# Second-transform points interleaved and rows moved in pairs, in a fused FFT convolution and recurrent-memory kernel

## Chip, cores and metric

The kernel runs on one core of a Trainium2 chip. The metric is the device time of one execution in microseconds (us); lower is better. Five runs of the kernel before have a median of 2174.39 us (2169.2 to 2178.17).

## What is computed

Two independent results stand side by side in the output, `out[0, s, 0:1024]` and `out[0, s, 1024:2048]`. Part A is a long convolution; part B is a recurrent attention with memory. Only A's data movement is changed. The reference, cut down:

```python
# A: S = 2048 positions, D = 1024 channels
k_shift = sum(k_pad[:, t:t+S, :] * shift_k[:, 3-t] for t in range(4))   # 4-tap causal filter
kv  = k_shift * v
y   = irfft(rfft(kv, 4096) * rfft(ssm_k, 4096))[:S]                     # long convolution per channel
a   = q * (y + kv * ssm_D)
# B: for each of 64 segments of 32 positions, with 8 memory rows in front
h = concat([mem, x[seg]]);  q, k, v = h@Wq, h@Wk, h@Wv                  # 32 heads of 128
o = softmax(mask(q k^T * scale)) v @ Wo;  mem = o[:8];  out = o[8:]
```

## The kernel before, in words

**Order of the work.** `b_kernel` opens with B's preparations and calls A inside them (L632, `run_a`). A has three stages; in between and after them B's weights are loaded and projections that don't depend on the recurrence are computed. The recurrent loop over 64 segments (L859) comes last, under a hand-written order (`tc.manual_schedule()`, L805). Outside that block the framework chooses the order of each engine's instructions; in the trace, for example, weight loads of L541 stand between A's stores of L211 on the SP queue.

**A's transform.** Position `s = 16 p + r`, with `p` the partition (0 to 127) and `r` the row within it (0 to 15). The 4096-point transform is split: a first transform over `p` (a 128x128 matmul with `F1h`), then a second one over 32 points, made of the 16 rows `r` and a half `h` (0 or 1, the two matrices `F1h[0]`, `F1h[1]`). Between the two, the data go through DRAM, because the second needs another partition layout: `SK1` (the kernel's transform) and `SU1` (the data's), both `[128, 32, 1024]` bf16, with frequency `m` outermost and the 32 points in the middle. In the text before, point `n = 16 h + r`.

**Stage 1** (L214 to L244), 16 iterations `t`, one row each. PE transposes eight blocks of `ssm_k` (L218), ACT copies them (`kt`, L220), `stage1(kt)` makes 4 matmuls (L208), ACT casts two PSUM tiles of 1024 columns into `s_sb` (L210, three buffers), and SP stores `s_sb` (512 KB) to `SK1` (L211). Meanwhile SP loads row `t` of k (`K0`, 256 KB, five buffers, L225), POOL loads row `t` of v (L228; for `t < 8` into the eight slots `pw` that later hold weights, afterwards into two `Vt` buffers), DVE makes seven operations (four products with `SH`, three sums, the product with v: L237 to L243), and `stage1(u)` does as above into `SU1`. The filter needs rows `t-3` to `t`; rows before 0 are rows 13 to 15 of the partition above, which are loaded into `Kx` (two buffers) each time that they are used, six times in all, each as a POOL memset of partition 0 and two loads of 112 and 15 partitions (L60 to L63). When a `pw` slot is free again, a weight chunk of 512 KB is loaded into it (`group`, L541), and for streamed chunks POOL copies it to the DRAM tensor `WS` (L543).

**Between 1 and 2**, `stage1_done` (L477) places twelve resident chunks `Wmid` and runs the projection `dense(0, 0)` on PE (L584).

**Stage 2** (L352 to L363): 17 sets, each gathering 256 KB pieces of `SK1` and `SU1` with the 32 points of four frequencies on 128 partitions (L276), two half-units of matmuls with `Mre`, `Mim`, complex products on DVE and POOL, the inverse with `Nre`, `Nim`, and a store to `SZ` (L284), laid out as `SK1`. After each half-unit `fill()` (L618) puts in one step of B's projections.

**Stage 3** (L369 to L382), 16 iterations: SP loads `zt` (both halves of point row `t`, 512 KB, L372) and row `t` of q (256 KB, L378; four buffers each), PE makes 4 matmuls with `G2h` into one of three PSUM tiles (L375), DVE multiplies with q (L380) into `ot` (three buffers), POOL stores the row (L381), and `fill()` follows.

**After A**, B's value projections (`vb_ps`, L701) run on PE while their weights and the resident ones come in, and their results go to DRAM (`VBD`, L705). Then the loop starts; it streams weights with loads of 512 KB in 4 KB runs (`wring<-WS`, L661).

**The layout that the change is about.** A row of 1024 bf16 is 2 KB. With `n = 16 h + r`, the two halves of a point row lie 32 KB apart in DRAM, so each partition's 4 KB in `sb` is stored as two runs of 2 KB:

```python
nc.sync.dma_start(scratch.rearrange("m (h r) d -> r m h d", h=2)[t], sb[:])
```

Of the kernel before, what the change touches and what calls it, by code (L numbers as in the profile page):

```python
# [9 lines left out]
BF = mybir.dt.bfloat16  # L10
F32 = mybir.dt.float32
I32 = mybir.dt.int32
ACT = mybir.ActivationFunctionType
ALU = mybir.AluOpType
# [17 lines left out]
def a_kernel(ctx: ExitStack, tc, q, k, v, shift_k, ssm_k, ssm_D, outa, slot4, slot16, stage1_done, fill):  # L32
    nc = tc.nc
    S, D = 2048, 1024
    NP = 34
    NS = 17
# [5 lines left out]
    SZ = dram.tile([128, 32, D], BF, name="SZ")  # L42
# [6 lines left out]
    Nre = const.tile([128, NS, 128], BF, name="Nre")  # L49
    Nim = const.tile([128, NS, 128], BF, name="Nim")  # L50

    def rows_view(ap2d, t):
        return ap2d.rearrange("(p r) d -> r p d", r=16)[t]

    def load_rows(dst, src2d, t, lag, eng):
        c = t - lag
        if c >= 0:
            eng.dma_start(dst, rows_view(src2d, c))
        else:
            nc.gpsimd.memset(dst[0:1, :], 0.0)  # L60
            rv = rows_view(src2d, 16 + c)
            eng.dma_start(dst[1:113, :], rv[0:112])
            eng.dma_start(dst[113:128, :], rv[112:127])  # L63

    with ExitStack() as c1:
        cw = c1.enter_context(tc.tile_pool(name="a_cw", bufs=1, side="right"))
        io = c1.enter_context(tc.tile_pool(name="a1_io", bufs=2, side="right"))
        k0pool = c1.enter_context(tc.tile_pool(name="a1_k0", bufs=5, side="right"))
        wk = c1.enter_context(tc.tile_pool(name="a1_wk", bufs=3, side="right"))
        ps_big = c1.enter_context(tc.tile_pool(name="a1_ps", bufs=2, space=PSUM))  # L70
        ps_t = c1.enter_context(tc.tile_pool(name="a1_pst", bufs=2, space=PSUM))
# [66 lines left out]
        p_odd = icol("p_odd", ALU.bitwise_and, 1)  # L138
# [37 lines left out]
        for hf in range(4):  # L176
            pt = ps_big.tile([128, 1024], F32, tag="big", name="sh_ps")
            for e in range(2):
# [4 lines left out]
        p_mod32 = icol("p_mod32", ALU.bitwise_and, 31)  # L183
        p_div64 = icol("p_div64", ALU.arith_shift_right, 6)
        p_x = icol("p_x", ALU.arith_shift_right, 5, ALU.bitwise_and, 1)
        nx = cw.tile([128, 1], F32, name="nx")
        nc.vector.tensor_tensor(out=nx[:], in0=p_mod32[:], in1=p_div64[:], op=ALU.mult)
        phr = cw.tile([128, 1], F32, name="phr")
        nc.vector.tensor_scalar(out=phr[:], in0=p_x[:], scalar1=-1024.0, scalar2=1024.0, op0=ALU.mult, op1=ALU.add)
        phi = cw.tile([128, 1], F32, name="phi")  # L190
# [8 lines left out]
        w_f = cw.tile([128, NS], F32, name="w_f")  # L199
        nc.vector.tensor_scalar(out=w_f[:], in0=w_i[:], scalar1=kp[:, 0:1], scalar2=None, op0=ALU.add)  # L200
        nc.vector.tensor_tensor(out=aN0, in0=w_f[:].unsqueeze(2).to_broadcast([128, NS, 32]),
                                in1=kcol_f[:, 0:32].unsqueeze(1).to_broadcast([128, NS, 32]), op=ALU.mult)
        def stage1(u_tile, t, scratch):
            sb = wk.tile([128, 2, 1024], BF, tag="s1_sb", name="s1_sb")
            for h in range(2):
                pt = ps_big.tile([128, 1024], F32, tag="big", name="s1_ps")
                for hf in range(2):
                    nc.tensor.matmul(pt[:, hf * 512:(hf + 1) * 512], lhsT=F1h[h][:, :],  # L208
                                     rhs=u_tile[:, hf * 512:(hf + 1) * 512], start=True, stop=True)
                nc.scalar.copy(sb[:, h, :], pt[:])  # L210
            nc.sync.dma_start(scratch.rearrange("m (h r) d -> r m h d", h=2)[t], sb[:])  # L211

        ktiles = {}
        for t in range(16):  # L214
            pt = ps_t.tile([128, 1024], BF, tag="ktp", name="k_tp")
            for db in range(8):
                src = KS[:, db, :].rearrange("p (n r) -> p r n", r=16)[:, t, :]
                nc.tensor.transpose(pt[:, db * 128:(db + 1) * 128], src, ident[:])  # L218
            kt = wk.tile([128, 1024], BF, tag="kt", bufs=2, name="kt")
            nc.scalar.copy(kt[:], pt[:])  # L220
            if t == 0:
                nc.vector.tensor_tensor(out=kt[0:1, :], in0=kt[0:1, :], in1=Drow[0:1, :], op=ALU.add)
            stage1(kt, t, SK1)
            K0 = k0pool.tile([128, 1024], BF, tag="K0", name="K0")
            load_rows(K0, k, t, 0, nc.sync)  # L225
            ktiles[t] = K0
            Vt = slot4()[:, 0:1024] if t < 8 else io.tile([128, 1024], BF, tag="Vt", name="Vt")[:]
            load_rows(Vt, v, t, 0, nc.gpsimd)  # L228
            acc = wk.tile([128, 1024], BF, tag="uacc", bufs=2, name="uacc")
            for li, lag in enumerate((3, 2, 1, 0)):  # L230
                if t - lag >= 0:
                    Kl = ktiles[t - lag]
                else:
                    Kl = io.tile([128, 1024], BF, tag="Kx", name="Kx")
                    load_rows(Kl, k, t, lag, nc.sync)
                if li == 0:
                    nc.vector.tensor_tensor(out=acc[:], in0=Kl[:], in1=SH[:, lag, :], op=ALU.mult)  # L237
                else:
                    pr = wk.tile([128, 1024], BF, tag="prod", bufs=2, name="prod")
                    nc.vector.tensor_tensor(out=pr[:], in0=Kl[:], in1=SH[:, lag, :], op=ALU.mult)  # L240
                    nc.vector.tensor_tensor(out=acc[:], in0=acc[:], in1=pr[:], op=ALU.add)
            u = wk.tile([128, 1024], BF, tag="u", bufs=2, name="u")
            nc.vector.tensor_tensor(out=u[:], in0=acc[:], in1=Vt, op=ALU.mult)  # L243
            stage1(u, t, SU1)  # L244

        for x, (M, n) in enumerate(((Mre, nxr), (Mim, nxi))):
            aM = phases(x).rearrange("p (a b) -> p a b", b=32)
            nc.vector.tensor_scalar(out=aM, in0=v_i, scalar1=p_mod32[:, 0:1], scalar2=n[:, 0:1], op0=ALU.mult, op1=ALU.add)
            nc.vector.tensor_scalar(out=aM, in0=aM, scalar1=4095, scalar2=None, op0=ALU.bitwise_and)
            for (r0, c0) in [(0, 0), (64, 32)]:  # L250
                act_sin(M[r0:r0 + 64, :, c0:c0 + 32], aM[r0:r0 + 64], 12, r0)
            nc.gpsimd.memset(M[32:64, 0, :], 0.0)
# [112 lines left out]
    with ExitStack() as c3:  # L365
        io = c3.enter_context(tc.tile_pool(name="a3_io", bufs=4, side="right"))
        wk = c3.enter_context(tc.tile_pool(name="a3_wk", bufs=3, side="right"))
        ps_big = c3.enter_context(tc.tile_pool(name="a3_ps", bufs=3, space=PSUM))
        for t in range(16):  # L369
            pt = ps_big.tile([128, 1024], F32, tag="big", name="y_ps")  # L370
            zt = io.tile([128, 2, 1024], BF, tag="zt", name="zt")
            nc.sync.dma_start(zt[:], SZ.rearrange("m (h r) d -> r m h d", h=2)[t])  # L372
            for hf in range(2):
                for h in range(2):
                    nc.tensor.matmul(pt[:, hf * 512:(hf + 1) * 512], lhsT=G2h[h][:, :],  # L375
                                     rhs=zt[:, h, hf * 512:(hf + 1) * 512], start=(h == 0), stop=(h == 1))
            qt = io.tile([128, 1024], BF, tag="qt", name="qt")
            load_rows(qt, q, t, 0, nc.sync)  # L378
            ot = wk.tile([128, 1024], BF, tag="ot", name="ot")
            nc.vector.tensor_tensor(out=ot[:], in0=pt[:], in1=qt[:], op=ALU.mult)  # L380
            nc.gpsimd.dma_start(rows_view(outa, t), ot[:])  # L381
            fill()  # L382


# [732 lines left out]
```

## Time and profile before

| what | us |
|---|---|
| median of five runs | 2174.39 |
| the profiled execution | 2176.56 |
| its span, first to last instruction | 2173.6 |
| stage 1: first and last store issued (L211) | 20.2 and 115.6 |
| stage 3: first load and last store issued (L372, L381) | 291.9 and 348.8 |
| first weight load of the loop on SP (L661) | 433.0 |
| DVE operation of 128x1024 in stage 1 (L241) | 0.680 |
| ACT cast of 128x1024 in stage 1 (L210) | 1.037 |
| store to SK / SU, issue to landing, median | 4.6 / 5.1 |
| load of a row of k / q / zt, issue to landing, median | 6.0 / 6.5 / 8.5 |

How to read the views: "busy" is the time in which an engine executes; the figure in brackets after it is the number of instructions. In a timeline line the first number is the start and the second the duration, and the square bracket at its end gives the idle time before it and what ended it. "SPq" and "POOLq" are the instruction queues of SP and POOL, which issue DMAs in order: an issue that waits holds up all behind it. In the DMA view q1 holds the transfers issued by SP, q10 those of ACT, q0 those of POOL; the share is the time that packets took, over 16 engines and the window. Pipelined operations overlap a little, so the step from one ACT cast to the next is about 0.91 us and from one DVE operation to the next about 0.60 us.

### The profile page before, as it was taken

The page shows a single profiled execution, that of the slowest core. Times are in us where ns is not written, and L with a number is a line of the kernel's source. Part 1 is how long each engine was busy: PE and PEld are TensorE (multiplying, and loading weights), DVE is VectorE, ACT ScalarE, POOL GpSimd, SP SyncE. Part 2 cuts the span into 40 slices and gives each one's busy share as a digit, 9 for nine tenths or more (in the row PEclk, how much of TensorE's full clock was granted, in tenths as well). Part 3 has the DMA queues.
Part 4 walks back from the last instruction along what each step waited for, and adds up shares of the span by engine and source line. Part 5 has one row for each costly group of instructions (what it writes and reads, how often), then busy time and mean ns, then how long its engine had stood idle before and what let it go on. Part 6 is the DMA issues. An engine that isn't in the chain of part 4 may idle for free. (4 is left out here: it accounts for less than half of the span.)

```text
span 2173.6 us, 81452 instructions
## 1 busy us (share of the span) xinstructions
PE 1737.9 (80%) x35636; PEld 929.5 (43%) x35636; DVE 872.7 (40%) x2686; ACT 648.2 (30%) x1139; POOL 436.7 (20%) x1131
## 2 busy tenths in 40 slices
PE   4688989777888878888788788888888878888776
PEld 2232334334444444444444444444444444444444
DVE  9927752123333333333333333333333333333332
ACT  8935521122222222222222222222222222222221
POOL 4013532301111111111111112111111111111111
PEclk9899999989999999999999999999999999999999
DMA  9998879999999999999999999999999999999996
GB/s 327 340 336 305 278 288 389 286 367 394 392 365 368 394 373 391 389 391 397 390 394 396 393 393 389 392 382 383 389 383 382 389 390 392 396 390 393 393 369 259
DMA packets 262572, 804.63 MB, mean 370 GB/s; under 512 B 52204, under 2 KB 52236, under 8 KB 262215
## 3 DMA queue, kind: packets, MB, share of 16 engines
q1 hardware_dynamic: 229880, 725.84, 87.7%
q0 software_dynamic: 27120, 63.11, 8.5%
q10 hardware_dynamic: 5216, 10.49, 1.3%
q8 instruction: 278, 4.55, 0.9%
q14 instruction: 78, 0.64, 0.1%
HBM read 739.92 MB, written 62.39 MB: 369 GB/s over the span
## 5 line engine op out<-in xcount | busy, mean ns | idle before, releaser
L893 PEld LDWEIGHTS <-rec 128*32 128x32 bf16 x12351 | 324.8, 96 | 479.6 <-issue 256.8
L893 PE MATMUL acc<-wring,rec 128*32 128x512 bf16 (+1 forms) x3777 | 376.3, 387 | 142.8 <-DMA wring<-WS 125.4
L902 ACT CAST qkv_sb<-acc 128x512 bf16<-128x512 f32 x384 | 224.8, 585 | 666.7 <-PE acc L893 666.7
L979 PEld LDWEIGHTS <-OT 128*32 128x32 bf16 x8192 | 217.9, 97 | 179.1 <-issue 152.0
L979 PE MATMUL yacc<-wring,OT 128*32 128x256 bf16 x3072 | 154.8, 276 | 98.0 <-DMA wring<-WS 58.7
L893 PE MATMUL acc<-Wmid,rec 128*32 128x512 bf16 x3072 | 227.5, 386 | 0.0
L893 PE MATMUL acc<-Wres,rec 128*32 128x512 bf16 x2816 | 222.5, 382 | 0.0
L995 DVE COPY KT<-tps 128x512 bf16<-128x512 bf16 x64 | 27.2, 425 | 307.3 <-PE tps L908 307.3
L839 PEld LDWEIGHTS <-OTB 128*16 128x16 bf16 x4096 | 105.0, 90 | 102.7 <-issue 92.4
L965 ACT CAST OT<-OTp 128x512 bf16<-128x512 f32 x128 | 74.9, 585 | 245.6 <-PE OTp L957 245.6
L966 DVE CAST OTB<-OTp 128x128 bf16<-128x128 f32 x128 | 37.3, 292 | 266.5 <-ACT OT L965 266.5
L794 POOL DMA_DIRECT2D rec<-REC x64 | 37.4, 585 | 521.5 <-issue 267.6
L745 DVE TENSOR_SCALAR wring<-OTp 128x384 int32<-128x384 int32 x126 | 112.2, 891 | 53.5 <-PE acc L893 45.1
L893 PE MATMUL acc<-pw,rec 128*32 128x512 bf16 x1536 | 130.4, 382 | 0.0
L869 POOL COPY KT<-rec 128x128 bf16<-128x128 bf16 x128 | 38.6, 302 | 437.6 <-PE SB L917 435.1
L854 POOL DMA_DIRECT2D out_dram<-YB x128 | 73.1, 577 | 232.8 <-DVE YB L852 228.2
L923 DVE TENSOR_REDUCE mx<-SB 128x5 f32<-128x200 f32 x128 | 47.1, 368 | 172.6 <-PE SB L917 172.6
L839 PE MATMUL SB<-wring,OTB 128*16 128x256 bf16 x1488 | 79.2, 275 | 36.3 <-DVE SB L818 30.2
L908 PE MATMUL tps<-ident,qkv_sb 128*128 128x128 bf16 x1024 | 101.2, 221 | 8.0 <-ACT qkv_sb L902 0.2
L908 PEld LDWEIGHTS <-qkv_sb 128*128 128x128 bf16 x1024 | 62.7, 97 | 104.8 <-ACT qkv_sb L902 64.8
L979 PE MATMUL yacc<-Wlate,OT 128*32 128x256 bf16 x2048 | 105.7, 275 | 2.1 <-issue 1.3
L1035 ACT CAST Y<-yacc 128x256 bf16<-128x256 f32 x64 | 23.8, 372 | 241.0 <-PE yacc L979 225.5
(231 smaller groups left out, 2675.6 us busy)
## 6 DMA issues: line engine op xcount, KB each, us to landing
wring<-WS SPq DMA_DIRECT2D x1216, 512.0 KB, 7.4
rec<-REC POOLq DMA_DIRECT2D x64, 192.0 KB, 6.2
SK<-s_sb SPq DMA_DIRECT2D x16, 512.0 KB, 4.6
SU<-s_sb SPq DMA_DIRECT2D x16, 512.0 KB, 5.1
Kg<-SK SPq DMA_DIRECT2D x32, 256.0 KB, 4.5
Ug<-SU SPq DMA_DIRECT2D x32, 256.0 KB, 6.1
REC<-stage POOLq DMA_DIRECT2D x16, 512.0 KB, 8.6
zt<-SZ SPq DMA_DIRECT2D x16, 512.0 KB, 8.5
```

What stands on the lines that cost most here:

```text
L745: nc.vector.tensor_scalar(out=dst, in0=src, scalar1=0, scalar2=None, op0=ALU.bitwise_or)
L794: nc.gpsimd.dma_start(rec[:], REC[:, s, :])
L839: nc.tensor.matmul(self.acc[32 * dq:32 * dq + W, x - o:y - o], lhsT=self.OTB[:, c, 4 * g + i, :], rhs=r, start=first and not self.seeded, ...
L854: nc.gpsimd.dma_start(bass.AP(outb.tensor, outb.offset + (SEG * NB * self.b + NX) * 2048 + 256 * dq, [[2048 * SEG, NB], [2048, 8], [1, 256 ...
L869: nc.gpsimd.tensor_copy(KT[:, :, :, 32:40], KBs[:, 128 * g:128 * g + 128].rearrange("p (c i t) -> p i c t", c=4, i=4))
L893: nc.tensor.matmul(self.acc[32 * c:32 * c + 32, x - 512 * c:y - 512 * c], lhsT=hT[:, kc, :], rhs=r, start=(kc == 0 and x == 512 * c), stop ...
L902: nc.scalar.copy(sb[:], self.acc[:])
L908: nc.tensor.transpose(tp[:, i * 128:(i + 1) * 128], sb[:, i * 128:(i + 1) * 128], ident[:])
L923: nc.vector.tensor_reduce(out=mx[:], in_=S, op=ALU.max, axis=AX.X)
L965: nc.scalar.copy(OT[:], o_view[:, :, :, 0:32])
L966: nc.vector.tensor_copy(OTB[:, :, 4 * g:4 * g + 4, 8 * j:8 * j + 8], o_view[:, :, :, 32:40])
L979: nc.tensor.matmul(yacc[32 * dq:32 * dq + 32, x - o:y - o], lhsT=OT[:, c, i, :], rhs=r, start=(h == 0 and x == o), stop=(h == 31), tile_po ...
```

## The change

It has five parts.

1. The 32 points of the second transform are numbered `n = 2 r + h`. The stores of stage 1 and the loads of stage 3 now see one run of 4 KB per partition. The matrices `M` and `N` are built with the permuted numbers (`p_n2`, `kn2`); this adds three small DVE operations for `p_n2`'s base, one more for `p_n2` and one for `kn2`, and no operation later on. The gathers and scatters of stage 2 keep their shapes.
2. k is loaded two rows at a time into `K0` of 4 KB (four buffers of two rows for five of one).
3. v is loaded two rows at a time: rows 0 to 11 into six `pw` slots, rows 12 to 15 into two `Vt` buffers of 4 KB. Slots 6 and 7 are no longer used for v.
4. q is loaded two rows at a time (two buffers of two rows for four of one), and the output is stored two rows at a time after the odd row (two buffers of two for three of one). In the output tensor the rows lie 4 KB apart, so its runs stay 2 KB.
5. The shifted rows 13 to 15 are loaded once into `Kx` `[128, 3, 1024]` with one memset and two loads, ahead of the loop.

The diff's core:

```diff
+        p_n2 = icol("p_n2", ALU.arith_shift_right, 1, ALU.bitwise_and, 15)
+        nc.vector.scalar_tensor_tensor(out=p_n2[:], in0=p_odd[:], scalar=16.0, in1=p_n2[:], op0=ALU.mult, op1=ALU.add)
+        nc.vector.scalar_tensor_tensor(out=kn2[:], in0=odd_f[:, 0:32], scalar=16.0, in1=half_f[:, 0:32], op0=ALU.mult,
+                                       op1=ALU.add)
...
-            nc.sync.dma_start(scratch.rearrange("m (h r) d -> r m h d", h=2)[t], sb[:])
+            nc.sync.dma_start(scratch.rearrange("m (r h) d -> r m h d", h=2)[t], sb[:])
...
+        Kx = cw.tile([128, 3, 1024], BF, name="Kx")
+        nc.gpsimd.memset(Kx[0:1], 0.0)
+        kx_src = k.rearrange("(p r) d -> p r d", r=16)[:, 13:16, :]
+        nc.sync.dma_start(Kx[1:113], kx_src[0:112])
+        nc.sync.dma_start(Kx[113:128], kx_src[112:127])
+        ktiles = {c: Kx[:, c + 3, :] for c in (-3, -2, -1)}
...
-            K0 = k0pool.tile([128, 1024], BF, tag="K0", name="K0")
-            load_rows(K0, k, t, 0, nc.sync)
-            ktiles[t] = K0
-            Vt = slot4()[:, 0:1024] if t < 8 else io.tile([128, 1024], BF, tag="Vt", name="Vt")[:]
-            load_rows(Vt, v, t, 0, nc.gpsimd)
+            if t % 2 == 0:
+                K0 = k0pool.tile([128, 2048], BF, tag="K0", name="K0")
+                nc.sync.dma_start(K0[:], pair_rows(k, t))
+                ktiles[t], ktiles[t + 1] = K0[:, 0:1024], K0[:, 1024:2048]
+                Vp = slot4(t // 2) if t < 12 else io.tile([128, 2048], BF, tag="Vt", name="Vt")
+                nc.gpsimd.dma_start(Vp[:], pair_rows(v, t))
...
-            nc.sync.dma_start(zt[:], SZ.rearrange("m (h r) d -> r m h d", h=2)[t])
+            nc.sync.dma_start(zt[:], SZ.rearrange("m (r h) d -> r m h d", h=2)[t])
...
-            qt = io.tile([128, 1024], BF, tag="qt", name="qt")
-            load_rows(qt, q, t, 0, nc.sync)
-            ot = wk.tile([128, 1024], BF, tag="ot", name="ot")
-            nc.vector.tensor_tensor(out=ot[:], in0=pt[:], in1=qt[:], op=ALU.mult)
-            nc.gpsimd.dma_start(rows_view(outa, t), ot[:])
+            if t % 2 == 0:
+                qt = io.tile([128, 2048], BF, tag="qt", bufs=2, name="qt")
+                nc.sync.dma_start(qt[:], pair_rows(q, t))
+                ot = wk.tile([128, 2048], BF, tag="ot", bufs=2, name="ot")
+            half = slice(1024 * (t % 2), 1024 * (t % 2) + 1024)
+            nc.vector.tensor_tensor(out=ot[:, half], in0=pt[:], in1=qt[:, half], op=ALU.mult)
+            if t % 2:
+                nc.gpsimd.dma_start(outa.rearrange("(p r) d -> p r d", r=16)[:, t - 1:t + 1, :],
+                                    ot[:].rearrange("p (r d) -> p r d", r=2))
```

## Prediction

> **What bounds the kernel now.** First the page: how long each kind of work lasts. Its second part cuts the span into 40 slices of 54 us.
>
> ```profile
> span 2173.6 us, 81452 instructions
> ...
> PE   4688989777888878888788788888888878888776
> ...
> DMA  9998879999999999999999999999999999999996
> ```
>
> From the ninth slice on (433 us) runs B's loop, with DMA at 9 throughout. No line of it is changed, so all that can move lies in the first 435 us: a fifth of the span, and only the part of it that sets when the loop starts. Next the windows of the stages, with busy time per engine, the granted clock, DMA share and GB/s:
>
> ```profile
> 32.00:116.10 84.10, 54.55 (x247) 22.92 (x245) 73.43 (x132) 75.38 (x85) 6.82 (x13) 0.86 0.96 337
> 116.10:144.50 28.40, 28.40 (x124) 12.37 (x123) 3.46 (x5) 5.85 (x10) 0.00 (x0) 0.94 0.91 329
> 144.50:288.00 143.50, 127.33 (x692) 42.71 (x692) 109.34 (x190) 79.63 (x151) 63.40 (x62) 0.96 0.83 285
> 288.00:348.00 60.00, 46.72 (x208) 19.57 (x206) 24.85 (x25) 5.27 (x9) 17.04 (x26) 0.89 0.98 367
> 348.00:405.00 57.00, 57.00 (x266) 25.85 (x265) 9.08 (x16) 12.87 (x22) 18.05 (x25) 1.00 1.02 359
> ```
>
> The columns after the length are PE, PEld, DVE, ACT, POOL. Stage 1 (first line) is ACT's: 75.4 of 84.1 us; DVE has 73.4, but its last product ends at 105.3 us and ACT's last copy at 116.05. Then PE is full in the dense projection, nearly full in stage 2, has 13 us of gaps in stage 3, and is full again to 405 us. So what a stage gives up is passed on to the loop's start, unless DMA holds it: in stage 3 and after it DMA is at 0.98 to 1.02. What fills ACT's 8.7 us of idle time in stage 1, and DVE's, is in the waits:
>
> ```profile
> ACT s_sb L210 <- DMA SU<-s_sb: 6.1, 6, 1.8
> ACT s_sb L210 <- issue: 1.1, 1, 1.1
> ...
> DVE prod L240 <- POOL coli L505: 1.4, 1, 1.4
> DVE uacc L237 <- DMA Kx<-in_A_k_dram: 1.0, 1, 1.0
> DVE prod L240 <- DMA K<-in_A_k_dram: 1.0, 2, 0.8
> DVE prod L240 <- DMA Kx<-in_A_k_dram: 1.0, 1, 1.0
> ```
>
> ACT waits six times, up to 1.8 us, for a store of `s_sb` to land before the buffer can be written again. Three buffers are filled in about 7.3 us, of which 1.8 is the filling, so a store may take 5.5 us; the median is 5.1. Which stores are late is seen on SP's queue:
>
> ```profile
> 75.86 0.56 SPq L58 DMA_DIRECT2D K<-in_A_k_dram  x1
> 76.51 0.80 SPq L541 DMA_DIRECT2D pw<-in_B_Wk_dram  x1
> 78.01 0.52 SPq L211 DMA_DIRECT2D SU<-s_sb  x1
> ```
>
> The store issued at 78.0 stands behind 256 KB of k and 512 KB of weights; ACT waits for it until 84.49 (1.44 us lost). Each of the six late stores has a load of 512 KB shortly in front.
>
> Stage 3, by its waits (PE's line, then DVE's):
>
> ```profile
> PE y_ps L375 <- DMA zt<-SZ: 7.8, 6, 2.2
> ...
> DVE ot L380 <- DMA qt<-in_A_q_dram: 10.5, 2, 9.1
> ```
>
> Is DMA full there because runs are short? The DMA view of 20 us of stage 3 (2 KB runs), then of 100 us of the loop (4 KB runs): packets, MB, share.
>
> ```profile
> q1 hardware_dynamic: 3024, 5.90, 77.5%
> ```
>
> ```profile
> q1 hardware_dynamic: 9668, 35.19, 92.0%
> ```
>
> Per MB that is 0.775 x 320 / 5.90 = 42.0 and 0.920 x 1600 / 35.19 = 41.8 us of one engine: as good as equal. The packet records of the trace are kinder: the median 2 KB packet on SP's queue took 84 ns, a 4 KB packet 159, so two short ones cost 168: 5% more.
>
> **What the Trainium skill says.** "DMA: Bandwidth & Descriptors", section "Why small descriptors are slow (HBM only)", gives about 3 cycles per packet beside one per 32 bytes, and finds joining descriptors worth it only at 256 B and below. Estimate from it: (2 x 67) / 131, 2.3% for 2 KB against 4 KB; the trace's two readings, 0.5% and 5%, stand around it. Same page, "Queues, rings and completion order": descriptors of one issuing engine are taken in ring order on each DMA engine; agrees with the late store above. Same page, "SWDGE vs HWDGE vs iDMA": POOL's transfers are put into packets of up to 4096 B. The trace agrees: between 20 and 36 us q0, with v in 2 KB runs, moves 2.34 MB in 703 packets, 3.3 KB each. So pairing rows of v and of the output changes no packet size; only SP's transfers gain.
>
> **The change part by part.**
>
> *4 KB runs, DMA time.* On SP's queue 32 stores of 512 KB, 16 zt loads of 512 KB and 4.2 MB each of k and q: 33.6 MB, 8192 pairs of packets. At 168 - 159 = 9 ns a pair over 16 engines: 4.6 us of DMA time, of which stage 3 (12.6 MB) has 1.7 and stage 1 2.9. In stage 3 DMA sets the pace, so 1.7 counts (0.2 if the views per MB are right). In stage 1 ACT sets it, so its 2.9 counts only through the waits for stores.
>
> *Stores and ACT.* The upper end is all 6.1 us of ACT's waits. A store is itself shorter by (16 x 84 - 8 x 159) = 0.07 us per engine, and less descriptor work: of 4.6 to 5.1 us nearly nothing. What counts is what stands in front. K loads become four up front and four of 512 KB, each free to go when DVE has read the pair's second row; v's slot comes free within a microsecond of that, so K pair, weights and then the SU store may come together: 1024 KB in front for 768, at 400 GB/s 0.65 us longer, four times: 2.6 us lost. Against it: k is in hand after the tenth iteration, v is loaded at the start (no 256 KB per iteration at 71 to 97 us), and two of eight weight loads (slots 6 and 7) may come earlier, so that late bursts are 256 KB lighter or absent. Bounds: 6.1 gained, 2.6 lost. I take 3.0 gained, half of the waits, since two of the three largest (1.44 at 84 us, 1.79 at 110; the other 1.62 at 46) lie late, where less is in front.
>
> *Kx once.* Six memsets (0.94 us) on POOL become one of three rows, about 2.8 us, at 10.6 us where POOL has nothing else but v; 1.5 MB of loads become 0.76. It takes away DVE's 1.0 + 1.0, and the 1.4 ahead of the last product with Kx, put down to POOL: 3.4 us. K pairs take 1.0 more. But DVE ends 10.7 us before ACT: nothing on the path. If the order puts filter before tables on DVE, ACT's sines come later, yet ACT has the same sum of work: 0.
>
> *Added DVE operations.* Five, of 0.06 us step each in the rows of `icol` (10.71 to 11.27): 0.3 us, on DVE: hidden by the same 10.7 us.
>
> *v in front.* All eight loads can go at once, 4.2 MB for 2.5 before 32 us; with K pairs (0.75 more), two weight chunks (1.0) and Kx (0.76 less) about 2.7 MB more. Between 20 and 36 us DMA moves 284 GB/s; at 400 there is room for 26 us x 0.116 = 3.0 MB. Just covered; without the cover, 0.5 MB cost 1.3 us. I take 0.
>
> *q and output in pairs.* Same bytes. A q pair can be asked for only when both rows of the old one are read: one iteration (60/16 = 3.75 us) later for its first row. An output pair leaves one iteration later for its even row; its buffer is needed two iterations after, as now. Bounds: 8 fewer issues on SP and POOL (0.34 and 0.54 each, not on the path), to 7.5 us lost (below). I take 0.
>
> Sum: -3.0 - 1.7 = -4.7 us on 2176.56, 2171.9 for the profiled execution. It lies 2.2 above the median of the runs shown; on that scale 2169.7.
>
> **Rivals.**
> - *The bytes cost the same* (0.22). 42.0 against 41.8 us per MB: runs of 2 KB are no burden, and the stores stay late because of what is in front. Then 0.2 of stage 3 and 1 of ACT's waits: 2173.2. For it: 402 GB/s in the 20 us of stage 3, 368 in the 100 us of the loop.
> - *The lump comes late* (0.26, slower). One mechanism: a pair waits for both rows and then stands as 512 KB in SP's ring. Its place is stage 3, where q landed up to 17.2 us after issue and DVE already waited 9.1 us for one row; there the prefetch shrinks from four iterations (15 us) to three (11). It decides where q's landing exceeds 11 us: the stretch at 317 to 331 us, two pairs, 2 x 3.75 = 7.5 us. In stage 1 the same lump eats the gain. With stage 3's 1.7: +5.8, 2180.2. Against it: PE has other work to fill in, and if DMA is full all the time, order costs little.
> - *All waits go* (0.12). ACT's 6.1 and the 1.1 of issue, with 1.7, and 1 of zt's waits: -9.9, 2164.5. For it: DVE, the only other engine near its limit, gets 4.4 us of slack.
>
> **How the numbers follow.** My forecast has 0.40. A measurement of this kernel can tell about 0.2%, 4.35 us: below 2170.0 is faster, above 2178.7 slower. Of the forecast's 0.40, 0.28 falls below 2170.0 and 0.12 within. Faster 0.28 + 0.12 = 0.40; same 0.12 + 0.22 = 0.34; slower 0.26. The range takes the forecast, the equal-bytes case and most of both outer ones: 2163 to 2181. The signs are split, so the likeliest case's own range: 2166 to 2173.
>
> **What would show it.** Right: waits of ACT for SU stores at 3 us or less, the last store near 112; q1's median packet in stage 3 at 159 ns and its us per MB down by 4 to 5%; the loop's first SP load near 428. Wrong: a wait of DVE on qt that has grown by whole iterations, K pair, weight load and SU store side by side on SP with a longer wait behind them, or a stage 1 that DVE ends.

## Result, and the profile after

The changed kernel takes 2186.86 us (median of 23 runs; 2178.56 to 2195.9) against 2174.37 for the kernel before (44 runs beside it): ratio 1.0057, interval 1.0045 to 1.0070, 12.5 us slower, where the forecast was 4.7 us faster. Its profiled execution took 2180.34 us, one of its shortest; the loop itself lasts 1740.6 us in the profile of before and 1730.6 in that of after, though none of its lines changed, so the two profiles are compared by the times at which the stages begin and end, and the totals by the ratio.

| event, us | before | after | difference |
|---|---|---|---|
| last store of stage 1 issued | 115.6 | 114.4 | -1.2 |
| first gather of stage 2 issued | 116.9 | 124.1 | +7.2 |
| first product of stage 2 on PE (`Kre_ps`) | 144.6 | 153.7 | +9.1 |
| first `zt` load of stage 3 issued | 291.9 | 300.8 | +9.0 |
| last output store of stage 3 issued | 348.8 | 360.4 | +11.6 |
| first weight load of the loop | 433.0 | 447.3 | +14.3 |

The page of the changed kernel (span, PE and DMA in 40 slices) and its windows, cut where its stages lie (PE, PEld, DVE, ACT, POOL busy; granted clock, DMA share, GB/s):

```profile
span 2177.9 us, 81351 instructions
...
PE   4687988878878878888888888888878878888886
...
DMA  9879879999999999999999999999999999999996
```

```profile
32.00:124.10 92.10, 50.37 (x236) 21.73 (x235) 69.64 (x127) 77.82 (x86) 14.86 (x8) 0.80 0.86 306
124.10:153.70 29.60, 28.97 (x124) 12.59 (x124) 3.46 (x5) 6.43 (x11) 0.00 (x0) 0.92 0.74 269
153.70:297.00 143.30, 125.51 (x692) 42.59 (x692) 109.46 (x190) 79.47 (x151) 63.50 (x62) 0.98 0.82 280
297.00:357.00 60.00, 45.30 (x200) 19.20 (x199) 22.78 (x23) 5.27 (x9) 13.89 (x18) 0.89 0.98 360
```

The first line is what grew: 8 us longer than the 84.10 of before, with 2.4 us more of ACT's work in it (77.82 for 75.38), so ACT stands idle 14.3 us in place of 8.7. The projection and stage 2 behind it last as long as before within 1.2 us. Three long waits are new, in the lists of PE and of ACT (total, times, longest):

```profile
PE xbt_ps L527 <- POOL ident masks.py:199: 10.6, 1, 10.6
PE kb_ps L586 <- ACT XBT L529: 9.9, 1, 9.9
```

```profile
ACT s_sb L205 <- DMA SU<-s_sb: 11.8, 3, 8.6
```

*The wait for `ident`.* This is the identity matrix with which PE transposes x for B's projection; GpSimd makes it by a memset and a select (TENSOR_SCALAR_AFFINE_SELECT). POOL's timeline, then DVE's around its end:

```profile
13.33 5.14 POOL L229 DMA_DIRECT2D pw<-in_A_v_dram  x6
18.47 1.28 POOL L229 DMA_DIRECT2D Vt<-in_A_v_dram  x2
...
25.09 0.21 POOL masks.py:197 MEMSET ident<- 128x128 bf16 x1
25.33 0.55 POOL L524 DMA_DIRECT2D pair<-in_B_x_dram  x1
25.89 18.06 POOL masks.py:199 TENSOR_SCALAR_AFFINE_SELECT ident<-ident 128x128 bf16<-128x128 bf16 x1
```

```profile
43.11 0.68 DVE L238 TENSOR_TENSOR prod<-K,SH 128x1024 bf16<-128x1024 bf16 x1
46.97 0.69 DVE L241 TENSOR_TENSOR u<-uacc,pw 128x1024 bf16<-128x1024 bf16 x1 [3.18 <-PE s_ps L203]
```

Before, the select took 0.36 us:

```profile
32.50 0.36 POOL masks.py:199 TENSOR_SCALAR_AFFINE_SELECT ident<-ident 128x128 bf16<-128x128 bf16 x1
```

It ran just behind a 1.4 us gap of DVE in its products with `Kx`, not in the gap itself: DVE was at work again from 32.01 us, and the product beside the select took 0.78 us for the usual 0.69. With `Kx` in hand DVE runs without a gap from 19.0 to 43.8 us, and the select ends when it pauses; it pauses because PE, which waits for `ident`, takes no more `u`. The Trainium skill, "SBUF — State Buffer", section "Who interferes with whom", says that a DVE instruction with two inputs from SBUF contends with a GpSimd instruction that reads SBUF, not with one that only writes. The lines agree: the memset, which writes, took 0.21 us in the midst of the same DVE work.

*The wait for the SU store.* It was issued at 28.82, and ACT goes on at 41.35; the longest landing of an SU store in the first 60 us is 12.4 us, for 5.4 before. The DMA view of the changed kernel from 20 to 42 us:

```profile
DMA packets 2388, 8.41 MB, mean 382 GB/s; under 512 B 272, under 2 KB 272, under 8 KB 2388
...
q0 software_dynamic: 1101, 3.95, 48.1%
...
SU<-s_sb SPq DMA_DIRECT2D x2, 512.0 KB, 12.3
```

Before, the same stretch moved 6.81 MB, 2.88 of them on q0, and its SU stores landed in 4.6 us. In POOL's timeline above all of v is issued by 19.75 us; before, the issues of v's first ten rows stood between the six memsets of `Kx`, which wait for `Kx`'s two buffers, and went out one to three at a time from 10.6 to 31.3 us. That pacing went with part 5.

*The wait behind the sines.* ACT's timeline:

```profile
112.41 1.96 ACT L205 CAST s_sb<-s_ps 128x1024 bf16<-128x1024 f32 x2
114.40 4.83 ACT L107 ACTIVATE Nre<-ints,pi_col 32x1088 bf16<-32x1088 int32 x4
119.24 4.83 ACT L107 ACTIVATE Nim<-ints,pi_col 32x1088 bf16<-32x1088 int32 x4
124.09 0.58 ACT L529 COPY XBT<-xbt_ps 128x512 bf16<-128x512 bf16 x1
```

The sines of `Nre` and `Nim`, 9.7 us, stand behind stage 1's last cast and ahead of the last copy of `XBT`, the transposed x that the projection needs. Before, ACT made them from 23.58 to 38.25, among the first casts, and PE stood at that time for want of the first `u` (ACT's lines, then PE's):

```profile
23.58 4.83 ACT L117 ACTIVATE Nre<-ints,pi_col 32x1088 bf16<-32x1088 int32 x4
28.43 3.62 ACT L117 ACTIVATE Nim<-ints,pi_col 32x1088 bf16<-32x1088 int32 x3
...
37.05 1.20 ACT L117 ACTIVATE Nim<-ints,pi_col 32x1088 bf16<-32x1088 int32 x1
```

```profile
30.62 1.89 PE L208 MATMUL s_ps<-u,F1h 128*128 128x512 bf16 x4 [8.45 <-DVE u L243]
```

DVE's phases for them (L256, L257 before) were done by 25.7 us; now they end at 106.8, behind the filter.

Four theories stand against each other. **Theory 1**: the hold of PE by `ident` is the cause. **Theory 2**: the late sines are. **Theory 3**: the pairs of stage 3 (and the 4 KB runs) are. **Theory 4** joins the first two: late sines cost only because a hold has eaten as much before. None of them has the SU store's own lateness. In the names below, a_ is the changed kernel with an edit, b_ the kernel before with one.

### The profile page after: what moved, and what is told of

Its sections match the earlier page's. It is cut to its first block, busy times and chain, and to the rows that moved or that the text cites. A ratio compares the mean times of both kernels' runs of the same rounds, so it can differ in the third digit from the quotient of the medians.

```text
span 2177.9 us, 81351 instructions
## 1 busy us (share of the span) xinstructions
PE 1727.8 (79%) x35636; PEld 926.6 (43%) x35636; DVE 872.4 (40%) x2691; ACT 647.6 (30%) x1139; POOL 446.2 (20%) x1110
## 5 line engine op out<-in xcount | busy, mean ns | idle before, releaser
L586 PE MATMUL kb_ps<-XBT,pw 128*128 128x512 bf16 x320 | 87.0, 399 | 14.7 <-ACT XBT L529 9.9
```

Of the source, the lines that this page charges most:

```text
L586: nc.tensor.matmul(ps[:], lhsT=ws[kc][:, hl * 128:(hl + 1) * 128], rhs=xbt(kc).rearrange("p s t -> p (s t)"), start=(kc == 0), stop=(kc == 7))
```

## Experiments

**a_ident, a_tab: take each suspect away.**

```diff
+    make_identity(nc, ident[:])            # a_ident: ahead of run_a, out of make_consts
     run_a(pw, slot16, stage1_done, fill)
```

a_tab moves the lines of the four tables, from `for x, (M, n)` to the last `act_sin`, ahead of `def stage1`.

> The changed kernel, only with stage 2's identity matrix (ident) made ahead of stage 1 in place of inside it; the sines of Nre and Nim stay behind stage 1 on ACT. Theory 1 (GpSimd's select of ident, 18.06 us long because VectorE has no gap left, holds PE and so ACT): the select takes about 0.4 us, PE's wait for ident (10.6) and ACT's 8.6 us wait at its third cast go, the dense projection begins near 116 us instead of 124.7, and the time falls by some 8.6 us to about 2178. Theory 2 (the late sines on ACT are what costs): the dense projection still begins at 124 to 125 us and the time stays at 2187.

> The changed kernel, only with the sines of Nre and Nim put ahead of the loop over t, so that ACT runs them early; the select of ident stays where it was. Theory 1: the select is still 10 to 20 us long and PE still waits some 10 us for ident, but ACT now has its 9.7 us of sines to do in that hole, so the dense projection begins near 116 us and the time is about 2178. Theory 2: the same gain of 9.7 us (2177). If the sines do not lie in the hole but ahead of it, Theory 1 says no gain (124 us, 2187) and Theory 2 still says 2177.

a_ident: 2187.72 us, 1.0052 (1.0033 to 1.0072), no gain to be seen; first gather at 125.2, as theory 2 had it. The select is short (0.28 us), but PE is held at the same place by a load of x, issued at 24.6 and landed 12.9 us later. PE's waits:

```profile
PE kb_ps L585 <- ACT XBT L528: 10.9, 1, 10.9
PE xbt_ps L526 <- DMA pair<-in_B_x_dram: 9.7, 1, 9.7
```

a_tab: 2182.42 us, 1.0035 (1.0017 to 1.0052), first gather at 114.2. The ratio is 0.0022 lower, 4.8 us and uncertain by some 5, where theories 1 and 2 had 9 to 10. The first gather overstates the gain: the projection starts only at 117.3, behind the last `XBT` copies, and stage 2's first product is at 147.3 (153.7 in the changed kernel, 144.6 before). Here the select still takes 14.46 us and holds PE for 6.5 and ACT for 7.1, but the sines lie in time that ACT would have lost, and the first SU store goes out at 36.4 and lands within 6.0 us:

```profile
22.00 4.83 ACT L107 ACTIVATE Nre<-ints,pi_col 32x1088 bf16<-32x1088 int32 x4
26.84 4.83 ACT L107 ACTIVATE Nim<-ints,pi_col 32x1088 bf16<-32x1088 int32 x4
```

So the select alone is not the cause, since another hold takes its place; and the place of the sines matters.

**a_kx, b_kx: part 5 undone, and part 5 alone.** a_kx loads `Kx` again at each use, with a memset and two loads; b_kx has the new block and takes `Kl = ktiles[t - lag]` always.

> The changed kernel without its part on the shifted k rows: they are loaded six times again, as before. Theory 1: VectorE's two or three gaps of 1 to 1.4 us near 27 to 32 us come back, the select of ident is short (under 2 us) again, the dense projection begins near 116 us, time about 2178. Theory 3 (the pairs in stage 3 and the 4 KB runs are what costs): no change, 2187.

> The kernel before with the one part on the shifted k rows, everything else as before. Theory 1: VectorE has no gap in its first 25 us of products, the select of ident is 10 us or longer, PE waits for it; what it costs is 8.6 us if ACT's sines do not fill the hole (about 2183) and as little as 0 if they do (2174). Theory 3: no change (2174), with a select under 1 us.

a_kx: 2172.17 us, 0.9998 (0.9974 to 1.0021). Undoing part 5 gives back the whole loss: the ratio falls by 0.0059, 12.8 us, uncertain by some 6. DVE has its gaps, the select takes 0.53 us, the sines run at 25.7 to 40.8. But it isn't simply the order of before: 27 of the projection's 128 matmuls are done by 116.6 us, for 4 before, so that the projection ends sooner, although the first gather is 1.9 us later than before (PE's timelines, of before and of a_kx):

```profile
116.10 28.53 PE L584 MATMUL kb_ps<-XBT,pw 128*128 128x512 bf16 x124 [1.73 <-ACT XBT L527]
```

```profile
116.62 21.96 PE L594 MATMUL kb_ps<-XBT,pw 128*128 128x512 bf16 x101
```

Stage 2's first product is at 138.5, 15.2 us earlier than in the changed kernel and 6.0 earlier than before. Part of the 12.8 us is this other order of PE. b_kx: 2179.46, 1.0027 (1.0009 to 1.0044): part 5 alone costs 5.9, uncertain by some 4. Its select slipped through in 0.72 us, and only `Nim` is late. ACT's timeline:

```profile
108.94 2.02 ACT L210 CAST s_sb<-s_ps 128x1024 bf16<-128x1024 f32 x2
110.99 4.83 ACT L117 ACTIVATE Nim<-ints,pi_col 32x1088 bf16<-32x1088 int32 x4
115.84 0.59 ACT L528 COPY XBT<-xbt_ps 128x512 bf16<-128x512 bf16 x1
```

Its v rows also go out at once, but they are 2.5 MB for 4.2, and its SU stores land within 5.9 us. The last one leaves at 111.0 and the sines end where stage 1 ended before: here the late table costs nothing at that point. `zt` is 3.4 us later: 1.3 are there at stage 2's first product (145.9), the rest arises in stage 2, where PE waits 8.5 us once for `X_sb` (4.2 before), which landed 10.9 us after its issue; the gathers and weights ahead of it on SP stand in another order.

**a_xbtv, a_ident_x: the copy behind the sines; x on SP.** a_xbtv gives the last `XBT` copy (tb 3, h 1) to `nc.vector`; a_ident_x is a_ident with `xq = [nc.sync, nc.sync]`.

> The changed kernel with one copy moved: the last of the eight XBT copies (ahead of the dense projection) is made by VectorE in place of ACT; orders of PE, GpSimd and SP are the same as in the changed kernel, the sines of Nre and Nim stay behind stage 1 on ACT, and PE's 10.6 us hold by ident stays. Theory 2 (the cost is that the dense projection waits behind 9.7 us of sines): PE's 9.9 us wait for XBT goes, the dense projection begins near 115 us instead of 124.7, stage 3's first load moves from 300.8 to 292 to 295, time 2178 to 2181. Theory 1 (the early hold of PE by ident is the cost, the sines only stand where ACT would be late anyway): the projection starts earlier but stops at full PSUM until the sines are done, stage 3's first load stays at 299 to 301, time 2187.

> The changed kernel with ident made ahead of stage 1 and with all four loads of x for the transposes issued by SP (two were GpSimd's, behind eight loads of v), so that nothing should hold PE early; the sines stay behind stage 1. Theory 1, widened (the hold of PE in the first 45 us is the cost, whoever causes it: ident 10.6 us in the changed kernel, the load of x 9.7 in the version with an early ident): the hold is under 2 us, ACT's 9 us idle stretch goes, the dense projection begins near 116 us, time about 2178. Theory 2 (ACT has a hole at the start that only the sines can fill): ACT is idle at other places instead, the dense projection begins at 122 to 125 us, time 2185 to 2188.

a_xbtv: 2186.68, 1.0057 (1.0035 to 1.0079). The projection starts at 113.6 and stops after 15 matmuls, since ACT, in its sines, empties no PSUM:

```profile
113.61 4.09 PE L586 MATMUL kb_ps<-XBT,pw 128*128 128x512 bf16 x15
125.45 4.75 PE L586 MATMUL kb_ps<-XBT,pw 128*128 128x512 bf16 x15 [7.74 <-ACT stage L575]
```

It is ACT's time that is late, not one copy. This is what theory 1 had on record for it, and theory 4 has too; theory 2's gain didn't come. a_ident_x: 2188.06, 1.0062 (1.0038 to 1.0086); PE still waits 7.9 us for x, which took 14.4 us to land, first gather at 123.4. It did not take the hold away.

**a_s3, b_s3: single rows of q and output in the changed kernel; pairs in the kernel before.**

> The changed kernel with single rows of q and of the output again (its fourth part undone); the orders of PE, ACT and VectorE are the same as in the changed kernel. Theory 3 (pairs cost in stage 3, by the two output buffers and by the q pairs): the wait of VectorE for the output store (6.0) goes and that for q (7.9) falls to 2 to 4, stage 3 from first load to last output store is 57 us instead of 59.6, time 2.6 us lower (2184). If stage 3 only waits elsewhere then (DMA full): 59.6 us and 2187.

> The kernel before with the fourth part alone: q loaded and the output stored in pairs of rows; the orders of PE, ACT and VectorE are those of before. Theory 3: stage 3 grows from 57.0 to 59.6 us, with a wait of VectorE for the output store that before does not have; time 2.6 us higher (2177). My prediction's rival of the late lump: 7.5 us (2182). No cost: 2174.

b_s3: 2178.54, 1.0021 (1.0007 to 1.0036), 4.6 us. Stage 3 lasts 60.2 us for 57.0. DVE's waits there (2.3 for the output before; q, 10.5 before, is gone from the list):

```profile
DVE ot L385 <- DMA out_dram<-ot: 7.8, 2, 5.0
```

By these waits it is the two output buffers that cost, not q; PE's waits for `zt` grew as well (11.9 us for 7.8), and pairs of q and pairs of the output were not run one without the other. a_s3: 2187.86, 1.0065 (1.0042 to 1.0088): stage 3 is 58.2 us for 59.6, but no gain is to be seen in the total; the run is too uncertain to tell that from the expected 2.6.

**a_xfirst, a_xfirst_tab, a_xall, a_ident_v, a_xp: attempts at late sines without a hold.** All have `ident` early. a_xfirst loads two blocks of x on SP ahead of `run_a`, a_xfirst_tab has early sines as well, a_xall loads all four, a_ident_v loads v in single rows again, a_xp loads the four blocks by GpSimd right ahead of v:

```diff
     def pw(k=None):
+        if not x_pre:
+            for tb in range(4):
+                if tb % 2 == 0:
+                    xt2 = pair()
+                x_pre[tb] = xt2[:, 1024 * (tb % 2):1024 * (tb % 2) + 1024]
+                nc.gpsimd.dma_start(x_pre[tb], x.rearrange("(tb s t) d -> tb s t d", s=16, t=SEG)[tb, :, NX:SEG, :])
```

> The changed kernel with ident made and the first two blocks of x loaded (by SP) ahead of stage 1, so that neither ident nor the load of x can hold PE in the first 45 us; the sines of Nre and Nim stay behind stage 1 on ACT. Theory 4 (a hold of PE costs ACT 8 to 10 us only because ACT has no sines left to do in it; sines behind stage 1 cost only because that time was lost before): the last SU store is issued near 105 us, the sines end near 115, the dense projection gets going near 116, time about 2178. Theory 2 (sines behind stage 1 cost by themselves): last SU store near 114, projection near 124, time 2187.

> As the version with ident and x ahead of stage 1, with the sines of Nre and Nim put ahead of the loop as well. Theory 4: no further gain in the end of stage 1 over either remedy alone (ACT has the same sum of work): dense projection near 114 to 116, time 2176 to 2180, within 2 us of the version without the early sines. Theory 2: 10 us below the version without the early sines.

> The changed kernel with ident made and all four blocks of x loaded (by SP) ahead of stage 1, so that none of them can hold PE later on; the sines of Nre and Nim stay behind all of stage 1's casts on ACT. Theory 4 (late sines cost only where ACT has lost as much before to a hold of PE): no wait of PE above 3 us between 25 and 45 us, last SU store near 105, sines' end near 115, stage 2's first gather near 115, time about 2178. Theory 2 (late sines cost by themselves): last SU store near 114, first gather near 124, time 2187.

> The changed kernel with ident made ahead of stage 1 and v loaded in single rows again (2.5 MB of v up front in place of 4.2), sines behind stage 1. If the v pairs are what makes the load of x late (issued at 24.6, landed at 37.5 us with ident early): PE's wait for x is under 3 us, last SU store near 106, first gather of stage 2 near 116, time about 2178. If not: wait of 8 to 10 us, first gather near 124, time 2187.

> The changed kernel with ident made ahead of stage 1 and all four blocks of x loaded by GpSimd just ahead of v, so that they come neither ahead of the filter's and the transform's first loads (as in the version that put them first on SP) nor behind v; the sines stay behind stage 1. Theory 4: no hold of PE above 3 us between 25 and 45 us, last SU store 104 to 107, sines' end and stage 2's first gather 114 to 117, time 2177 to 2180. Theory 2 (late sines cost by themselves): last SU store near 114, first gather near 124, time 2187.

None came out as theory 4 has it. a_xfirst: 2185.54, 1.0051 (1.0036 to 1.0067); the transposes of blocks 0 and 1 moved ahead, and block 2, 8.7 us late, holds PE in their place. a_xfirst_tab: 2181.42, 1.0026 (1.0013 to 1.0040), first gather 116.7 for 125.5, stage 2's first product 146.6 for 153.2: early sines are worth 0.0025 here, 5.4 us. a_xall: 2183.85, 1.0051 (1.0029 to 1.0073); x in front made the filter's taps late, so that ACT began 7 us later. a_ident_v: 2193.28, 1.0071 (1.0045 to 1.0098); x still 5.7 us late. a_xp: 2189.19, 1.0076 (1.0049 to 1.0103); x is there, and PE is held by a weight, ACT by an SU store that was issued at 31.60 and landed 12.4 us later. The timelines of a_xp:

```profile
45.19 1.03 PE L592 MATMUL kb_ps<-XBT,pw 128*128 128x512 bf16 x2 [9.30 <-DMA pw<-in_B_Wk_dram]
```

```profile
44.05 1.93 ACT L205 CAST s_sb<-s_ps 128x1024 bf16<-128x1024 f32 x2 [8.80 <-DMA SU<-s_sb]
```

The common ground is DMA: from 8 to 40 us its share is 1.02 to 1.04 in the changed kernel (0.89 to 1.04 before), and what is issued between 22 and 33 us, be it x, a weight or a store, lands 10 to 14 us later, before 4 to 6. With early sines the first SU stores are issued at 34 to 38 us (42.8 in a_xall_tab_s3), when the jam is over; ACT has made its tables while it lasted. In a_ident_v, with 2.5 MB of v up front, they land in 5.6 us or less, but v's later rows bring the waits for stores back (7.1 us in total), and the sines are late all the same. So the jam by itself is not what the total follows.

**b_4k, a_kx_s3, a_xall_tab_s3, a_xp_tab_s3: what the rest is worth.** b_4k is the kernel before with part 1; a_kx_s3 has parts 1 to 3 only; the last two are a_xall and a_xp with early sines and single rows in stage 3, part 5 kept.

> The kernel before with the 4 KB runs alone (its points renumbered). My prediction: 1.7 us gained in stage 3 and part of 3.0 at ACT's waits for stores, 2170 to 2173. Rival of equal bytes: 2174, with the packets of 4 KB taking 159 ns for two of 84. Theory of the order: VectorE's gaps stay, ident is short and the sines lie within stage 1, so nothing is lost: not above 2175.

> The changed kernel without its part on the shifted k rows (loaded six times, as before) and with single rows of q and of the output: 4 KB runs and pairs of k and v are what is left of the change. If single rows give back what the pairs cost in the kernel before (4.6 us), 2168; if they give nothing, as in the changed kernel, 2172 (the version with the pairs and without the part on the shifted rows). Stage 3 from first load to last output store 57 instead of about 59 us.

> All remedies on the changed kernel: ident and x ahead of stage 1, sines ahead of the loop, single rows of q and of the output; the shifted rows stay loaded once. Theory 4: stage 2's first gather near 112 to 115, stage 3 57 us, time 2170 to 2174. If what is left of the change costs by its order alone (x loads of stage 2, weights in front): 2178 to 2181.

> As the version with x ahead of v on GpSimd, with the sines of Nre and Nim ahead of the loop and single rows of q and of the output. Theory 4: first gather of stage 2 at 110 to 115, stage 3 57 us, time 2168 to 2173, so as fast as the kernel before or a little faster. If parts of the change other than hold, sines and stage 3's pairs cost: 2178 or more.

b_4k: 2175.82, 1.0004 (0.9990 to 1.0019). Its DMA view of 20 us of stage 3, queue of SP:

```profile
q1 hardware_dynamic: 2102, 5.80, 76.2%
```

0.762 x 320 / 5.80 = 42.0 us of one engine per MB, as before with 2 KB runs, at 397 GB/s for 402. This one window flatters the rival: q is still loaded in 2 KB runs here, and over the whole of stage 3 the figure is 42.3 (295 to 352 us) for 43.4 (292 to 349), 2.6% less. But stage 3 lasts 57.0 us in both, so the longer runs bought no time there. The total neither shows the predicted gain of 1.7 us or more nor excludes the smallest of it. a_kx_s3: 2171.07, 0.9990 (0.9974 to 1.0006). a_xall_tab_s3: 2179.20, 1.0013 (0.9999 to 1.0026), with a_xall's late start. a_xp_tab_s3: 2173.47, 1.0008 (0.9986 to 1.0031): against a_xp, early sines and single rows in stage 3 are worth 0.0068, 14.8 us, and the loss is gone, or not to be seen, although part 5 is in (x ahead of v is in both). No version beats the kernel before by more than the measurement is uncertain.

**b_probe: the lock by itself.** In the kernel before, after the filters of t = 5 and 7:

```diff
             stage1(u, t, SU1)
+            if t in (5, 7):
+                scr = wk.tile([128, 128], BF, tag="scr", bufs=1, name="scr")
+                nc.vector.tensor_copy(scr[:], u[:, 0:128])
+                make_identity(nc, scr[:])
```

> The kernel before with two probes: after the filters t = 5 and t = 7 VectorE copies 128 columns of u to a tile of its own, then GpSimd sets that tile (a memset, which only writes) and runs the select on it (which reads); nobody waits for either. If GpSimd's reading of SBUF is locked out while VectorE runs operations with two inputs from SBUF back to back: memset 0.2 us, select several us, ending where VectorE pauses. If the 18 us of the changed kernel have another reason: both under 0.6 us.

POOL's timeline:

```profile
58.61 0.21 POOL masks.py:197 MEMSET scr<- 128x128 bf16 x1 [10.55 <-DVE scr L247]
58.89 9.44 POOL masks.py:199 TENSOR_SCALAR_AFFINE_SELECT scr<-scr 128x128 bf16<-128x128 bf16 x1
68.28 0.56 POOL L547 DMA_DIRECT2D WS<-pw  x1
68.83 0.22 POOL masks.py:197 MEMSET scr<- 128x128 bf16 x1
69.13 0.78 POOL masks.py:199 TENSOR_SCALAR_AFFINE_SELECT scr<-scr 128x128 bf16<-128x128 bf16 x1
```

The first select waits until DVE itself stops, for the tile that the select holds; the second slips in after 0.78 us, beside a DVE sum that took 0.78 us for the usual 0.68. So a select can be held until DVE stops, and how long it is held varies. One execution, 2176.13 us, beside 2176.65 for before.

**All together**, sorted by the place of the sines of `Nre` and `Nim` (times in us from each kernel's one profile):

| kernel | sines | ACT busy, 16 to 48 | longest SU landing to 60 us | last SU store | first gather | stage 3 | ratio |
|---|---|---|---|---|---|---|---|
| after | behind | 19.4 | 12.4 | 114.4 | 124.1 | 59.6 | 1.0057 |
| a_ident | behind | 17.8 | 12.0 | 115.5 | 125.2 | 60.0 | 1.0052 |
| a_xbtv | behind | 19.4 | 12.6 | 115.1 | 124.8 | 59.0 | 1.0057 |
| a_ident_x | behind | 19.9 | 11.2 | 113.7 | 123.4 | 58.5 | 1.0062 |
| a_s3 | behind | 19.1 | 11.9 | 114.6 | 124.3 | 58.2 | 1.0065 |
| a_xfirst | behind | 22.4 | 12.3 | 115.8 | 125.5 | 59.7 | 1.0051 |
| a_xall | behind | 26.8 | 9.2 | 114.0 | 122.5 | 58.8 | 1.0051 |
| a_ident_v | behind | 21.8 | 5.6 | 117.2 | 126.9 | 58.2 | 1.0071 |
| a_xp | behind | 21.5 | 12.4 | 116.8 | 126.5 | 59.0 | 1.0076 |
| b_kx | half | 29.7 | 5.9 | 111.0 | 115.8 | 56.6 | 1.0027 |
| a_tab | within | 23.4 | 6.0 | 113.6 | 114.2 | 59.6 | 1.0035 |
| a_xfirst_tab | within | 27.4 | 4.2 | 115.8 | 116.7 | 60.7 | 1.0026 |
| b_s3 | within | 28.8 | 5.4 | 115.6 | 116.7 | 60.2 | 1.0021 |
| a_xall_tab_s3 | within | 31.3 | 6.9 | 121.3 | 121.9 | 58.4 | 1.0013 |
| a_xp_tab_s3 | within | 27.0 | 7.8 | 111.7 | 112.6 | 57.5 | 1.0008 |
| b_4k | within | 25.5 | 6.8 | 116.6 | 117.1 | 57.0 | 1.0004 |
| a_kx | within | 25.1 | 8.9 | 118.0 | 118.7 | 59.2 | 0.9998 |
| a_kx_s3 | within | 24.9 | 8.4 | 117.6 | 118.4 | 57.7 | 0.9990 |
| before | within | 28.6 | 5.4 | 115.6 | 116.9 | 57.0 | 1 |

All nine kernels with both tables behind stage 1 lie above all eight others with an edit and both tables within it; a single pair (after and a_tab, a_xfirst and a_xfirst_tab) is at the edge of its uncertainty. Four of the eight lack part 5; the four that have it (1.0008 to 1.0035) still lie below the nine. The last store leaves at a median of 115.1 us with both tables behind and of 115.8 with both within (before among them): taking 9.7 us of sines out of stage 1 does not end it sooner, it only puts them behind it. Stage 3 averages 59.4 us with pairs (12 kernels) and 57.5 with single rows (7).

## Why the prediction was wrong, point by point

- **"If the order puts filter before tables on DVE, ACT's sines come later, yet ACT has the same sum of work: 0."** This step failed. The order did that, and ACT's sum is the same (92.2 us from 14 us to the first gather, 93.2 before), but a stage ends by work and holes. Before, the sines lay at 23 to 38 us, where PE could not feed ACT (it waited 8.5 us for the first `u`); behind the last cast they hold the projection, and the first gather came 7.2 us later, stage 2's first product 9.1. In place of 0, putting the sines early gave 4.8 us (a_tab) and 5.4 (a_xfirst_tab) of the total, and the whole of part 5 measured 12.8 us when undone, another order of PE included, and 5.9 alone.
- **What bounds stage 1.** "Stage 1 is ACT's" was read from 75.4 us busy of 84.1 from 32 us on. Its start was not looked at as a stage of its own; there the first data rule.
- **v in front, "just covered", 0.** The second step that failed. The working asked whether the mean rate has room for 2.7 MB more (it had: DMA moved 412 GB/s from 24 to 32 us for 290), not how long a single store then takes to land: 12.4 us for 5. ACT stood 8.6 us for it. (That room was read from 284 GB/s between 20 and 36 us; the engines' busy share there was 0.92 already.) What the jam costs by itself no run shows: with less of it, a_ident_v was not faster. The pacing by the memsets of `Kx` on POOL, which part 5 removed, was not seen either, though the prediction lists them.
- **Kx once, DVE's 3.4 us of gaps**: they went, and "nothing on the path" was right for DVE, which ends at 104.2 for 105.3. What was missed is that GpSimd's select, which ran just behind one of the gaps, found no opening without them (in b_kx it did, 0.72 us). In the changed kernel it ends 2.6 us after the late store has landed, so little of the loss is its own; in a_tab it holds ACT for 7.1 us.
- **4 KB runs, 1.7 us in stage 3**: no time gained (57.0 us in both). The rival of equal bytes had the time right and the bytes not quite: over stage 3 a MB cost 2.6% less in b_4k, near the estimate of 2.3%, and below the 5% of the packet records (84 and 159 ns) that the 1.7 us came from. The Trainium skill's "DMA: Bandwidth & Descriptors", "Why small descriptors are slow (HBM only)", finds joining worth it only at 256 B and below; b_4k's ratio of 1.0004 agrees.
- **Stores and ACT, 3.0 us**: the waits for SU stores fell as forecast, 6.1 to 3.2 us in b_4k, but the last store left at 116.6, not 112: ACT then waited for PE (2.8) and for phases from DVE (2.5). A wait removed in this stage is replaced by another.
- **q and output in pairs, 0**: mis-sized. b_s3 measured 3.2 us in stage 3 and 4.6 in total. Of the rival "the lump comes late" the stage and the sign held for b_s3, the mechanism did not: DVE did not wait longer for q, it waited for one of two output buffers. The rival's "slower" for the whole kernel came true mostly by the late sines in stage 1, which it did not have: that is luck.
- **Added DVE operations, 0**: nothing seen of them.

Shown: part 5 brings the loss, or most of it; with it come the late sines, the jam of DMA and the held select, not each of them every time (in b_kx one table is late and the select short); putting the sines' text ahead brings stage 2's first product back from 153 to 154 us to 144 to 147 in three pairs, and about 5 us of the total in each of the two that differ in nothing else. In the fourth, a_xall and a_xall_tab_s3 with their late start, it stays (149.7 and 151.0). How the rest of the 12.5 us divides among the jam, stage 3's pairs and the order of the loads is not shown. Argued only: that late sines would be free if nothing were late in the first 45 us. b_kx speaks for it with one table; every attempt with both met another late transfer, and a version with paced v and late sines wasn't run. Open too is why the stretch between stage 3 and the loop took 2.7 us more: the granted clock of that one execution was 0.90 there for 0.94.

## What to carry to other kernels

Before taking a wait or a buffer recycle away, list what it had paced or made room for: transfers queued behind it, table work that a scheduler had put into the gap, an engine that could work only in the gap. A table made in a start-up hole can be free, and the same table behind the last tile can hold up what follows: 9.7 us of sines here cost about 5 of the total. An engine's busy sum bounds a stage only where the engine has no holes, so cut the start of a stage off as a window of its own. When loads are moved to the front, look at the landing time of what is issued behind them, not only at mean bandwidth.

## What was unexpected of the hardware

A 128x128 select on GpSimd that reads SBUF took 0.28 to 0.78 us where DVE paused or let it in, and 9.44, 14.46 and 18.06 us beside back-to-back DVE operations with two SBUF inputs; memsets of such a tile took 0.20 to 0.22 us throughout. A load of 256 KB needed 12.9 us (GpSimd's queue, behind v) and 14.4 us (SP's queue, which had no v on it) while DMA ran full, for 4.2 otherwise. And runs of 4 KB in place of 2 KB made a MB 2.6% cheaper for the DMA engines over stage 3 (42.3 for 43.4 us of one engine) without making the stage shorter.
